# Weight decoding in block 0: cast and split of a piece in one turn, and four attention steps at other places

## The chip, the cores and the metric

The kernel runs on one core of one Trainium2 chip. The metric is the device time of one launch in microseconds (us). TensorE is PE in the profile, VectorE is DVE, ScalarE is ACT, GpSimd is POOL, and SyncE, which issues all the transfers here, is SP. Each of them works through its own queue in order and waits for the others at semaphores.

## What is computed

Three stages follow each other: linear attention over 8 batches of 8 heads (576 tokens, head width 64), a feed-forward layer with `h - tanh(h)`, and a second one with a rational function. The change touches the first two.

```python
q_s = softmax(q, over the 64 entries of a head)
k_s = softmax(k, over the 576 tokens)          # needs the maximum of each column of k
kv  = einsum('bhsd,bhse->bhde', k_s, v)
x   = einsum('bhsd,bhde->bhse', q_s, kv)       # then reshaped to 4608 tokens x 512
h   = x @ w_in                                 # 512 -> 2048
x   = (h - tanh(h)) @ w_out                    # 2048 -> 512
...                                            # second layer: g = P(h) / (Q(h) + 1e-6)
```

## The kernel before

**Blocks and steps.** The 4608 tokens are 9 blocks of 512. The first layer takes 16 steps a block (144 in all, numbered n). Step n forms one 128 x 512 tile `hps` of `h` (`first_product`, 12 matmuls over 4 chunks of 128, each product split in three: high by high, low by high, high by low), takes `t = tanh(hps)` on ACT (L978) and the difference `hps - t` on DVE (L981, called the difference below), rounds it to its high part `gh` on ACT (L336) and forms the rest `gl = g - gh` (L340; on DVE in block 0, on POOL later). Two steps later (`LAG1`) 12 matmuls add it into the four banks `acc` (`second_product1`). There are two `hps` buffers in PSUM. In block 0 the difference is written over `hps` itself, so `hps` of step n comes free for step n + 2 only when `gl` of step n is formed; from block 1 on it is written into `t` in SBUF.

**Decoding.** The weights come as 64-bit floats. In block 0 and shortly before it, 32 pieces of 128 x 512 are decoded (order: a0, a1, b0, a2, b1, a3, ..., a for `w_in`, b for `w_out`). A call of `decode` is a turn; a turn opens one piece (two ACT instructions, L131 and L133, and L134 on DVE), joins the piece opened a turn ago (L146 and L147 on DVE), and handles the one joined before: `dec_high` casts it to the high part on ACT (L154) and `dec_low` splits off the low part (L158), on DVE in a step's first turn and on POOL in its second. In the kernel before, the cast stands last in the turn on ACT, and the split follows one turn later, behind DVE's opening. A step of block 0 has two turns, one ahead of L340 and one behind it; steps 2 and 6 have one. Seven turns lie ahead of step 0.

**Attention steps.** The attention of batch b is cut into four head pairs, and each of its steps is put by hand into a table `work[n]` (L713 to L739). Plain functions stand at the start of step n (`front`, L945), pairs of functions are done where PE turns to them behind the products of step n (`turn`, L976), and their second half behind L340 (`follow`, L990). For keys the steps are `kv_max` (L456 and L457, L461 from batch 2 on), then in batch 1 a transpose on PE with the maximum over it (`kv_turn`, L468; `kv_top`, L474), the way back and the subtraction (`kv_back`, L479; `kv_sub`, L485), the exponential (L495) and the product with the values (`kv_mm`, L515). From batch 2 on the maximum goes through `kv_squares` (L540, L542), a store and a broadcast fetch through memory and `kv_join` (L556). For queries they are `q_max` (L590, DVE), `q_sub` (L595, POOL), `q_exp` (L605, ACT), `q_sum` (L610 to L612 on DVE and L613 on POOL), and the product with `kv` (L660), which ACT copies into `xr` (L674). Behind step 15 `next_x` casts `xr` to `xh` on ACT (L320) and forms `xl` on DVE (L322), on which the first product of block 1 waits.

**Order.** Nothing but the program's own order sets an engine's order (`manual_schedule`). Transfers wait in SP's queue in the order in which they are written.

Of the kernel before, what the change touches and what calls it, by code (L numbers as in the profile page):

```python
# [43 lines left out]
def attention_moe_moe2_kernel(ctx, tc, q, k, v, w1, w2, w3, w4, ca, cb, out):  # L44
# [31 lines left out]
    def f32(ap):  # L76
        return ap.bitcast(F32)
# [27 lines left out]
    staged, joining, parting = [], [], []  # L105
# [43 lines left out]
    def place(piece):  # L149
        which, f = piece  # L150
        return [w[:, f % 4, :] for w in wsl[which, f // 4]]

    def dec_high(piece, m):
        ACT.copy(out=place(piece)[0], in_=f32(m))  # L154

    def dec_low(piece, m, on_dve):
        hi, lo = place(piece)
        (DVE if on_dve else POOL).tensor_tensor(out=lo, in0=f32(m), in1=f32(hi), op=ALU.subtract)  # L158

    def dec_start():  # L160

        old = [joining.pop()] if joining else []
        if staged:
            piece, t = staged.pop(0)
            if wide:
                joining.append((piece, t, *dec_open(t)))
            else:
                old.append((piece, t, None, t))
        return old

    def dec_end(ph, old, low_on_dve):
        if parting and parting[0][2]:
            dec_low(*parting.pop(0)[:2], low_on_dve)
        for x in parting:
            dec_high(*x[:2])
            x[2] = True
        if wide:
            for _, _, e, m in old:
                dec_join(e, m)
        parting.extend([piece, m, False] for piece, _, _, m in old)  # L180
        fetch_w(ph)

    def decode(ph, low_on_dve):
        dec_end(ph, dec_start(), low_on_dve)


# [520 lines left out]
    def put(s, fn, *args):  # L707
        work[max(s, 0)].append((fn, args))

    def first(j):  # L710
        return (j - 1) * KF

    kv_at = {(1, p): 3 * p + 4 for p in range(NPAIR)}  # L713
    q_at = {(1, p): (7, 10, 13, 14)[p] for p in range(NPAIR)}
    for j in range(2, NBLK):
        for p in range(NPAIR):
            q_at[j, p] = first(j) + (8, 8, 14, 14)[p]
            if j < B:
                kv_at[j, p] = first(j) + (8 if p > 1 else 2 if j == 2 else -2)
    q_from = {(j, p): (1, 3, 6, 9)[p] if j == 1 else at - (7 if p % 2 else 10) for (j, p), at in q_at.items()}  # L720
    kv_from = {(b, p): at - (1 if b > 1 and p % 2 else 2) for (b, p), at in kv_at.items()}
    for j in range(1, NBLK):
        for p in range(NPAIR):
            if j < B:
                s, at = kv_from[j, p], kv_at[j, p]
                steps = (s - (2 if p else 1), s - 1, s, s + 1, at) if j == 1 else (s - 3, s - 3, s - 1, s, s, s, at)
                for fn, s in zip(KV if j == 1 else KV_LATER, steps):
                    put(s, fn, j, p)
            s, at = q_from[j, p], q_at[j, p]
            steps = (s - 1, s, s + 1, s + 2, at - 2, at) if j == 1 else (s - 1, s, s + 1, s + 2, s + 3, s + 5, at)  # L730
            for fn, s in zip(Q if j == 1 else Q_LATER, steps):
                put(s, fn, j, p)
        for p in range(2, NPAIR + 2):
            to, before = (j + p // NPAIR, p % NPAIR), (j + (p - 2) // NPAIR, (p - 2) % NPAIR)
            if to in kv_at:
                put(kv_from[before] + 1, load_k, *to)
                put(kv_at[before] + 1, load_v, *to)
            if to in q_at:
                put(q_from[before] + 2, load_q, *to)  # L739

    with tc.manual_schedule():
# [200 lines left out]
        for n in range(STEPS):  # L942
            j, f = n // KF, n % KF
            leave = None
            front(work[n])  # L945
            flush()
            hps = first_product(f)
            if f == KF - 1 and j + 1 < NBLK:
                next_x()
            if n == last:  # L950
                ACT.activation(out=absb, in_=coef[:, 4:6], func=AF.Abs)
                DVE.tensor_scalar(out=coef[:, 0:4], in0=coef[:, 0:4], scalar1=-1.0, scalar2=None, op0=ALU.mult)
            if n == last + 10:
                for errand in todo:
                    for _ in errand:
                        flush()
                flush()
                for pool in (att, bdp, decp, rawp):
                    pool.release()
                outp = ctx.enter_context(tc.tile_pool(name="outp", bufs=4, side="right"))  # L960
                rp = ctx.enter_context(tc.tile_pool(name="rp", bufs=2, side="right"))
                xup = ctx.enter_context(tc.tile_pool(name="xup", bufs=1, side="right"))
                units = [xup.tile([P, NB], F32R, tag=f"u{k}", name=f"u{k}") for k in range(12)]
                units += [w[:, c, :] for w in (xh, xl) for c in range(KC)]
                sums = xup.tile([P, NB], F32, tag="sums", name="sums")
                top = xup.tile([P, HALF], F32, tag="top", name="top")
                temp = xup.tile([P, NB], F32, tag="temp", name="temp")
                for u in range(6):
                    load_unit(0, u)
            if n in due:  # L970
                leave = due.pop(n)()
            if n >= last + LAG1:
                unpark("b", f - LAG1)
            if n > last and f % 4 == 0:
                ring(f // 4 - 1)
            after = turn(work[n])  # L976
            t = gp.tile([P, NB], F32, tag="t", name="t", bufs=1)
            ACT.activation(out=t, in_=hps, func=AF.Tanh)  # L978

            g = t if j else hps  # L980
            DVE.tensor_tensor(out=g, in0=hps, in1=t, op=ALU.subtract)  # L981
            ph_w, turns = None, 0
            if j == 0:
                ph_w, turns = 0, 1 if f in (2, 6) else 2
            gh, gl = split_high(g)
            due[n + LAG1] = lambda a=(j, f, gh, gl): second_product1(*a)
            if turns:
                decode(ph_w, True)
            split_low(g, gh, gl, POOL if j else DVE)
            follow(after)  # L990
            if leave:
                leave()
            if turns > 1:
                decode(ph_w, False)
            if n == KF:
                fetch_w(1)
            if n > KF:
                for errand in todo:
                    next(errand, None)
            if n == STEPS - 1:  # L1000

                ACT.activation(out=ahead, in_=bias_q, func=AF.Abs_reciprocal_sqrt)
# [17 lines left out]
        steps = {f"P{m}": lambda i, m=m: product(i, m) for m in UNITS}  # L1020
# [51 lines left out]
```

## Time and profile before

| | |
|---|---|
| median of 3 runs | 1656.37 us (1656.07 to 1657.74) |
| profiled execution, device time | 1659.01 us |
| its span, first to last instruction | 1657.2 us |
| PE, DVE, ACT, POOL busy, share of the span | 97%, 67%, 62%, 63% |
| PE's granted clock, mean of the span | 0.995 of full |

The profiled execution took 1659.01 us, of which 1657.2 us are the span between its first and its last instruction. The changed places lie in the first 200 us of the span: the attention of block 0 until about 36 us, block 0 of the first layer until about 143 us, and the first steps of block 1. Shares of the whole span say little on them; they are read from stretches of that part, from the list of PE's waits in it and from the instructions in order of time.

### The profile page before, as it was taken

How to read it: one execution, taken by the hardware profiler on the slowest of the kernel's cores; microseconds unless marked ns; L12 is line 12 of the kernel's file. 1: busy time of each engine (PE TensorE's matmuls, PEld its weight loads, DVE VectorE, ACT ScalarE, POOL GpSimd, SP SyncE). 2: the span in 40 equal slices, each digit the busy share in tenths (PEclk: the TensorE clock that was granted, in tenths of full speed). 3: DMA queues.
4: the chain of work that ended last, by engine and by line, in shares of the span. 5: the costliest groups of instructions: out<-in, count | busy, mean ns of one | idle time of the engine just before them, and what ended most of it. 6: DMA issues, size and time to landing. Idle time of an engine off the chain costs nothing.

```text
span 1657.2 us, 26929 instructions
## 1 busy us (share of the span) xinstructions
PE 1613.7 (97%) x9400; PEld 1375.9 (83%) x9400; DVE 1111.3 (67%) x1839; ACT 1023.7 (62%) x1821; POOL 1039.3 (63%) x876
## 2 busy tenths in 40 slices
PE   5899999999999999999999999999999999999998
PEld 3677788888888888887888999898999899999996
DVE  7997656575565656361214787878787787878786
ACT  5675554544545545443325777777777777777775
POOL 4223637375553727273434888888888778778775
PEclk9999999999999999999999999999999999999999
DMA  8563765667473766352387585858686757676640
GB/s 233 174 189 88 208 181 173 182 172 210 135 215 113 222 167 198 107 165 65 121 308 292 173 281 191 291 191 296 196 293 203 267 204 255 214 246 220 209 141 26
DMA packets 250728, 323.75 MB, mean 195 GB/s; under 512 B 119008, under 2 KB 185568, under 8 KB 241376
## 3 DMA queue, kind: packets, MB, share of 16 engines
q1 hardware_dynamic: 250592, 322.03, 61.2%
q8 instruction: 74, 1.21, 0.3%
q14 instruction: 62, 0.51, 0.1%
HBM read 249.04 MB, written 72.93 MB: 194 GB/s over the span
## 4 chain that ended last, share of the span: by engine, by line
PE 86%; DVE 6%; ACT 3%; DMA 3%; issue 1%; SPq 1%; POOL 1%; DVEq 0%; ACTq 0%; POOLq 0%
PE acc L80 14%; PE acc L81 14%; PE acc L82 14%; PE z L866 12%; PE y L866 9%; PE hps L80 7%; PE hps L81 7%; PE hps L82 7%; PE kvps L515 1%; PE xps L660 1%; DVE m L134 1%; DMA u<-x2d 1%; DVE m L147 1%; DMA xh<-x2d 1%; DVE e L146 1%
## 5 line engine op out<-in xcount | busy, mean ns | idle before, releaser
L340 POOL TENSOR_TENSOR gl<-t,gh 128x512 fp32r<-128x512 f32 x128 | 174.5, 1363 | 301.8 <-ACT gh L336 275.8
L923 POOL TENSOR_TENSOR n<-n,r 128x512 f32<-128x512 f32 x144 | 186.3, 1294 | 97.8 <-ACT r L920 92.5
L981 DVE TENSOR_TENSOR t<-hps,t 128x512 f32<-128x512 f32 x128 | 88.1, 689 | 233.0 <-ACT t L978 232.9
L336 ACT CAST gh<-t 128x512 fp32r<-128x512 f32 x128 | 79.7, 622 | 250.3 <-PE acc L82 143.2
L923 POOL TENSOR_TENSOR n<-n,n 128x512 f32<-128x512 f32 x144 | 186.7, 1296 | 36.5 <-ACT n L907 36.5
L923 POOL TENSOR_TENSOR n<-n,h 128x512 f32<-128x512 f32 x144 | 187.6, 1303 | 9.6 <-DMA xl<-x2d 9.6
L978 ACT ACTIVATE t<-hps 128x512 f32<-128x512 f32 x144 | 86.0, 597 | 118.9 <-PE hps L82 86.2
L877 ACT COPY sums<-z 128x256 f32<-128x256 f32 x144 | 53.8, 373 | 134.7 <-PE z L866 134.7
L903 ACT ACTIVATE n<-h,coef 128x512 f32<-128x512 f32 x144 | 116.6, 810 | 0.3 <-POOL n L923 0.3
L933 DVE CAST gh<-a 128x512 fp32r<-128x512 f32 x144 | 99.6, 692 | 16.1 <-PE z L866 0.5
L936 DVE TENSOR_TENSOR gl<-a,gh 128x512 fp32r<-128x512 f32 x144 | 99.6, 692 | 15.5 <-DVE gh L933 0.9
L929 DVE SCALAR_TENSOR_TENSOR a<-a,n 128x512 f32<-128x512 f32 x144 | 100.0, 695 | 14.3 <-POOL n L923 8.5
L912 DVE SCALAR_TENSOR_TENSOR a<-h,absb,a 128x512 f32<-128x512 f32 x144 | 107.6, 747 | 3.0 <-ACT a L897 2.9
L897 ACT ACTIVATE a<-h,coef 128x512 f32<-128x512 f32 x144 | 100.5, 698 | 2.8 <-DVE gl L936 2.8
L926 DVE SCALAR_TENSOR_TENSOR a<-a,r 128x512 f32<-128x512 f32 x144 | 99.4, 690 | 0.8 <-ACT r L920 0.8
L915 ACT ACTIVATE r<-a,bias_q 128x512 f32<-128x512 f32 x144 | 97.1, 674 | 0.0
L920 ACT ACTIVATE r<-r 128x512 f32<-128x512 f32 x144 | 91.1, 632 | 4.6
L900 ACT ACTIVATE h<-h 128x512 f32<-128x512 f32 x144 | 89.2, 619 | 1.0 <-DMA xh<-x2d 0.8
L884 DVE TENSOR_TENSOR h<-y,sums 128x256 f32<-128x256 f32 x72 | 30.6, 425 | 58.4 <-PE y L866 58.4
L888 DVE TENSOR_TENSOR h<-y,top 128x512 f32<-128x512 f32 x72 | 49.7, 691 | 26.5 <-ACT top L877 24.3
L613 POOL TENSOR_TENSOR qe<-qe,qs 128x512 f32<-128x512 f32 x36 | 40.6, 1127 | 40.4 <-DVE qs L612 40.4
L80 PE MATMUL acc<-wb3h,gh 128*128 128x512 f32 x144 | 56.9, 395 | 2.9 <-DVE gh L933 2.9
(296 smaller groups left out, 5114.9 us busy)
## 6 DMA issues: line engine op xcount, KB each, us to landing
u<-x2d SPq DMA_DIRECT2D x78, 256.0 KB, 5.3
raw<-in_moe_w_in_dram SPq DMA_DIRECT2D x32, 512.0 KB, 4.3
raw<-in_moe_w_out_dram SPq DMA_DIRECT2D x32, 512.0 KB, 4.4
x2d<-raw SPq DMA_DIRECT2D x64, 256.0 KB, 3.6
x2d<-xr SPq DMA_DIRECT2D x56, 256.0 KB, 4.0
wa0h<-wa0d SPq DMA_DIRECT2D x9, 1024.0 KB, 5.0
wa1h<-wa2d SPq DMA_DIRECT2D x9, 1024.0 KB, 5.0
wa2h<-wa4d SPq DMA_DIRECT2D x9, 1024.0 KB, 5.1
```

The lines of the kernel that those rows point to most:

```text
L80: PE.matmul(o, lhi, rhi, start=start, stop=False)
L81: PE.matmul(o, lhi, rlo, start=False, stop=False)
L82: PE.matmul(o, llo, rhi, start=False, stop=stop)
L340: eng.tensor_tensor(out=gl, in0=g, in1=f32(gh), op=ALU.subtract)
L866: PE.matmul(o, w, x[:, xc], start=m in (1, 5) and c == k == 0, stop=c == 1 and k == 2, skip_group_check=True,)
L897: ACT.activation(out=new(t, "a", ps_a), in_=t["h"], func=AF.Abs, scale=b0)
L903: ACT.activation(out=new(t, "n1"), in_=t["h"], func=AF.Identity, scale=a3, bias=a2)
L912: DVE.scalar_tensor_tensor(out=t["a"], in0=t["h2"], scalar=b1, in1=t["a"], op0=ALU.mult, op1=ALU.add)
L923: return lambda t: POOL.tensor_tensor(out=t[a], in0=t[a], in1=t[b], op=op)
L929: DVE.scalar_tensor_tensor(out=t["a"], in0=t["a"], scalar=2.0, in1=t["n0"], op0=ALU.subtract, op1=ALU.mult)
L933: DVE.tensor_copy(out=t["g"][0], in_=t["a"])
L936: DVE.tensor_tensor(out=t["g"][1], in0=t["a"], in1=f32(t["g"][0]), op=ALU.subtract)
```

## The change

- **Decoding.** The cast now stands first in a turn on ACT, ahead of the opening's two instructions (`dec_top`), and the split follows in the same turn, behind DVE's join, where it used to follow a turn later. DVE still takes the split of a step's first turn and POOL that of the second; since the split is a turn earlier, the `a` pieces of the early steps now fall to DVE and the `b` pieces to POOL.
- **First pair of batch 1.** Its maximum, transpose, way back and query steps (`q_max`, `q_sub`, ...) move a step later: `kv_max` and `kv_turn` from step 1 to 2, `kv_back` to 3, the exponential to 4, `q_max` from 0 to 2. Its product stays in step 4. The loads that reuse its buffers move by a step too.
- **Batch 2.** The first two `kv_max` move from steps 13 and 14 to 15 and 16, the products from 18 to 19; the query steps of its first pair move two steps later (`q_max` from 13 to 15, `q_exp` from 15 to 17).
- **Step 0.** Its difference is written to `t` in SBUF as in later blocks, so its `hps` comes free right behind the difference.

```diff
+    def dec_top():
+
+        for x in parting:
+            dec_high(*x)
+
     def dec_end(ph, old, low_on_dve):
-        if parting and parting[0][2]:
-            dec_low(*parting.pop(0)[:2], low_on_dve)
-        for x in parting:
-            dec_high(*x[:2])
-            x[2] = True
         if wide:
             for _, _, e, m in old:
                 dec_join(e, m)
-        parting.extend([piece, m, False] for piece, _, _, m in old)
+        while parting:
+            dec_low(*parting.pop(0), low_on_dve)
+        parting.extend((piece, m) for piece, _, _, m in old)
         fetch_w(ph)
 
     def decode(ph, low_on_dve):
+        dec_top()
         dec_end(ph, dec_start(), low_on_dve)
...
-                kv_at[j, p] = first(j) + (8 if p > 1 else 2 if j == 2 else -2)
-    q_from = {(j, p): (1, 3, 6, 9)[p] if j == 1 else at - (7 if p % 2 else 10) for (j, p), at in q_at.items()}
+                kv_at[j, p] = first(j) + (8 if p > 1 else 3 if j == 2 else -2)
+    q_from = {(j, p): (2, 3, 6, 9)[p] if j == 1 else at - (7 if p % 2 else 8 if at == 24 else 10) for (j, p), at in q_at.items()}
...
-                steps = (s - (2 if p else 1), s - 1, s, s + 1, at) if j == 1 else (s - 3, s - 3, s - 1, s, s, s, at)
+                steps = (s - 2, s - 1, s, s + 1, at) if j == 1 and p else (s, s, s + 1, at, at) if j == 1 else (s - 3 + (at == 19), s - 3 + (at == 19), s - 1, s, s, s, at)
...
-            steps = (s - 1, s, s + 1, s + 2, at - 2, at) if j == 1 else (s - 1, s, s + 1, s + 2, s + 3, s + 5, at)
+            steps = (s - (p > 0), s, s + 1, s + 2, at - 2, at) if j == 1 else (s - 1, s, s + 1, s + 2, s + 3, s + 5, at)
...
-                put(kv_from[before] + 1, load_k, *to)
+                put(kv_from[before] + (2 if before == (1, 0) else 1), load_k, *to)
...
-            g = t if j else hps
+            g = t if j or not n else hps
```

Three places show how the queues change. From L187 on, a line of the changed kernel has a number three greater than the same line of the kernel before.

The first is DVE's queue around the maximum of batch 1's first pair (`mx<-kt`), from that maximum on in the kernel before, where it stands ahead of the difference of step 1:

```order
L456 TENSOR_TENSOR mx<-kt_158 128x256
L457 TENSOR_TENSOR mx<-mx,kt_158 128x128
L981 TENSOR_TENSOR hps<-hps,t 128x512
L134 TENSOR_SCALAR m<-raw 128x512
L158 TENSOR_TENSOR wb0l<-m,wb0h 128x512
L146 TENSOR_SCALAR e<-e 128x512
L147 ISA m<-e,m 128x1024
L340 TENSOR_TENSOR gl<-hps,gh 128x512
L474 TENSOR_REDUCE mc<-kvps 128x1
```

And in the changed kernel, from `gl` of step 1 on:

```order
L343 TENSOR_TENSOR gl<-hps,gh 128x512
L134 TENSOR_SCALAR m<-raw 128x512
L146 TENSOR_SCALAR e<-e 128x512
L147 ISA m<-e,m 128x1024
L459 TENSOR_TENSOR mx<-kt_158 128x256
L460 TENSOR_TENSOR mx<-mx,kt_158 128x128
L593 TENSOR_REDUCE qm<-qr 128x8 x2
L984 TENSOR_TENSOR hps<-hps,t 128x512
```

The maximum has moved behind the whole of step 1, two query maxima stand with it, and the split stands behind the join in a first turn.

The second is ACT's queue in step 7, from `gh` on; first the kernel before:

```order
L336 CAST gh<-hps 128x512
L131 ACTIVATE e<-raw 128x512
L133 ACTIVATE m<-raw 128x512
L154 CAST wa2h<-m 128x512
L674 COPY xr<-xps 64x256 x4
L527 ACTIVATE bd_115<-xps,rs 128x64
L131 ACTIVATE e<-raw 128x512
L133 ACTIVATE m<-raw 128x512
L154 CAST wb2h<-m 128x512
```

Then the changed kernel, from the same place:

```order
L339 CAST gh<-hps 128x512
L154 CAST wa2h<-m 128x512
L131 ACTIVATE e<-raw 128x512
L133 ACTIVATE m<-raw 128x512
L677 COPY xr<-xps 64x256 x4
L530 ACTIVATE bd_115<-xps,rs 128x64
L154 CAST wb2h<-m 128x512
L131 ACTIVATE e<-raw 128x512
L133 ACTIVATE m<-raw 128x512
```

The cast that POOL's next split waits for was the fourth row (`wa2h`); now it is the seventh (`wb2h`), behind the four copies.

The third is DVE's queue at the end of block 0; first the kernel before, from the last join on:

```order
L147 ISA m<-e,m 128x1024
L461 TENSOR_REDUCE mx<-kt_159 128x128
L540 STREAM_TRANSPOSE mx<-mx 128x128
L542 TENSOR_REDUCE mc<-mx 128x4
L981 TENSOR_TENSOR hps<-hps,t 128x512
L158 TENSOR_TENSOR wb3l<-m,wb3h 128x512
L340 TENSOR_TENSOR gl<-hps,gh 128x512
L322 TENSOR_TENSOR xl<-xr,xh 128x512 x4
```

Then the changed kernel, from `gl` of step 14 on:

```order
L343 TENSOR_TENSOR gl<-hps,gh 128x512
L464 TENSOR_REDUCE mx<-kt_158 128x128
L543 STREAM_TRANSPOSE mx<-mx 128x128
L545 TENSOR_REDUCE mc<-mx 128x4
L593 TENSOR_REDUCE qm<-qr 128x8
L325 TENSOR_TENSOR xl<-xr,xh 128x512 x4
L984 TENSOR_TENSOR hps<-hps,t 128x512
L343 TENSOR_TENSOR gl<-hps,gh 128x512
```

Of the two maxima of batch 2 one now stands between `gl` of step 14 and the four `xl` of block 1, the other behind them.

## Rows read from the trace of the kernel before

**Rows 1.** Windows by stretch: from:to, length, busy PE, PEld, DVE, ACT, POOL, clock, DMA.

```profile
42.30:50.20 7.90, 0.02 (x1) 0.00 (x0) 7.72 (x13) 4.47 (x8) 2.45 (x2) 0.77 0.54 159
...
54.00:112.00 58.00, 58.00 (x339) 46.68 (x338) 54.72 (x103) 43.61 (x82) 15.22 (x13) 1.00 0.61 185
...
144.00:149.00 5.00, 4.78 (x15) 3.71 (x15) 4.29 (x7) 2.85 (x6) 0.00 (x0) 0.66 0.00 0
```

**Rows 2.** PE's waits, 30 to 240 us: total us, times, longest.

```profile
PE kvps L468 <- DVE mx L456: 7.9, 1, 7.9
...
PE xps L660 <- ACT xr L674: 2.1, 1, 2.1
PE hps L80 <- ACT xh L320: 1.3, 1, 1.3
...
PE qps L619 <- ACT bd L527: 1.0, 1, 1.0
```

**Rows 3.** DVE in order of time, steps 0 to 4: start, duration, line.

```profile
43.21 0.69 DVE L981 TENSOR_TENSOR hps<-hps,t 128x512 f32<-128x512 f32 x1
...
46.41 1.47 DVE L134 TENSOR_SCALAR m<-raw 128x512 uint16<-128x512 uint16 x1
...
49.77 0.42 DVE L456 TENSOR_TENSOR mx<-kt 128x256 f32<-128x256 f32 x1
...
50.43 0.69 DVE L981 TENSOR_TENSOR hps<-hps,t 128x512 f32<-128x512 f32 x1
...
56.83 0.69 DVE L981 TENSOR_TENSOR hps<-hps,t 128x512 f32<-128x512 f32 x1
...
68.99 0.69 DVE L981 TENSOR_TENSOR hps<-hps,t 128x512 f32<-128x512 f32 x1
```

**Rows 4.** POOL in order of time, splits and query subtractions of block 0.

```profile
39.63 1.61 POOL L158 TENSOR_TENSOR wa0l<-m,wa0h 128x512 fp32r<-128x512 f32 x1 [1.52 <-ACT wa0h L154]
...
47.52 1.23 POOL L595 TENSOR_TENSOR qe<-qr,qm 128x512 f32<-128x512 f32 x1
...
80.83 1.24 POOL L595 TENSOR_TENSOR qe<-qr,qm 128x512 f32<-128x512 f32 x1
91.07 1.29 POOL L158 TENSOR_TENSOR wa2l<-m,wa2h 128x512 fp32r<-128x512 f32 x1 [9.01 <-ACT wa2h L154]
...
135.40 1.33 POOL L595 TENSOR_TENSOR qe<-qr,qm 128x512 f32<-128x512 f32 x1
```

**Rows 5.** ACT in order of time, step 7.

```profile
88.68 0.59 ACT L336 CAST gh<-hps 128x512 fp32r<-128x512 f32 x1 [0.82 <-DVE hps L981]
...
90.87 1.53 ACT L674 COPY xr<-xps 64x256 f32<-64x256 f32 x4
92.44 0.32 ACT L527 ACTIVATE bd<-xps,rs 128x64 f32<-128x64 f32 x1
```

**Rows 6.** DVE in order of time, step 7 and the end of block 0.

```profile
87.89 0.70 DVE L981 TENSOR_TENSOR hps<-hps,t 128x512 f32<-128x512 f32 x1 [0.84 <-ACT t L978]
...
92.78 0.46 DVE L134 TENSOR_SCALAR m<-raw 128x512 uint16<-128x512 uint16 x1
...
94.18 0.68 DVE L610 TENSOR_REDUCE qs<-qe 128x8 f32<-128x512 f32 x1
...
128.55 1.29 DVE L461 TENSOR_REDUCE mx<-kt 128x128 f32<-128x640 f32 x1
...
131.02 0.69 DVE L981 TENSOR_TENSOR hps<-hps,t 128x512 f32<-128x512 f32 x1
...
135.86 1.42 DVE L147 CUSTOM_DVE_ANT_0 m<-e,m 128x1024 uint16<-128x1024 uint16 x1
...
139.08 0.69 DVE L981 TENSOR_TENSOR hps<-hps,t 128x512 f32<-128x512 f32 x1
...
143.55 2.50 DVE L322 TENSOR_TENSOR xl<-xr,xh 128x512 fp32r<-128x512 f32 x4 [2.38 <-ACT xh L320]
```

**Rows 7.** Transfers of the batch 2 maxima (`kd`), steps 13 to 22, issue to landing.

```profile
DMA to landing us min/median/max: 1.4/3.4/7.2
```

## The prediction

> **What bounds the kernel now.** I read the stretches of the first 180 us first [rows 1]. From 42.3 to 50.2 us PE does nothing at all while DVE is busy for 7.72 of 7.90 us; from 54 to 112 us PE shows no idle time at the full clock, and DVE is busy for 54.72 of 58.00 us; from 144 to 149 us PE runs at a granted clock of 0.66. Then the list of PE's waits [rows 2]: 7.9 us for the maximum of batch 1's first pair, which stands between two products in PE's queue, 2.1 us for the copies of step 13, 1.3 us for `xh` of block 1, 1.0 us behind step 10. Together 12.3 us, and this is the pot that the change is aimed at. The question is what PE meets when a wait goes, so I read DVE's instructions in order of time [rows 3]. The differences of steps 0, 1, 2 and 4 start at 43.21, 50.43, 56.83 and 68.99 us, and DVE stands idle nowhere between them. So DVE sets the pace of the early steps, and PE's 7.9 us are mostly its lead over DVE: what does not shorten DVE's queue moves that wait and does not remove it.
>
> What stretches DVE's queue is POOL. An opening on DVE takes 0.46 us alone [92.78, rows 6] and 1.47 us where it meets a split on POOL [46.41, rows 3]; a join is held for 1.42 us and ends at 137.28, 0.55 behind POOL's subtraction (135.40 + 1.33) [rows 4, 6]. The other way round POOL waits for DVE's running instruction and then goes ahead of DVE's next one: the split at 39.63 takes 1.61 us where others take 1.29 [rows 4].
>
> The Trainium skill, page "SBUF — State Buffer", section "SBUF: two separate sides", says that VectorE and GpSimd share one pair of ports as an exclusive lock, held for a whole instruction by the one that starts first. By that rule each collision costs in full, which speaks against moving POOL's split behind DVE's opening; the trace agrees (1.47 against 0.46 us), and what the rule makes of the time stands with the second rival.
>
> **Steps 0 to 3.** The sum goes by the start of DVE's differences. Ahead of step 0 a `q_max` (0.6 us) leaves DVE's queue, but ACT's cast of b1 now stands ahead of two openings and waits for its join, so tanh comes later: I take 43.4 against 43.21. A first turn with difference, opening, split, join and `gl` takes 46.41 - 43.21 = 3.2 us [rows 3]; the new order has the same five parts, and the cast on ACT comes in time for a split behind the join, so 3.2 stays. The second turn of step 0 took 49.77 - 46.41 = 3.36 us with two POOL instructions against it, the split and the `q_sub` at 47.52 [rows 3, 4]; now only the split: 1.40 for a turn that nothing holds [92.78 to 94.18, rows 6] and 1.15 for one hold, 2.55. Step 1 then starts at 43.4 + 5.75 = 49.15 and ends at 54.9. Only there stands the moved maximum (0.66, the 50.43 - 49.77 of rows 3): it is ready at 55.6. PE forms `hps` of step 2 from 44.0 (step 0's buffer is free behind the difference: this edit works), adds step 0 into `acc` until about 49.5 (24 matmuls of 0.23), and waits at the transpose until 55.6: **6.1 us in place of 7.9**. Two query maxima (1.2) put step 2 at 56.8, where it was 56.83. Nothing is won. In step 2 the two `q_sub` now run back to back against opening and join, about 1.3 us by the same kind of hold; with the maximum and 0.33 for `kv_top` step 3 starts at 62.2, and with 3.2 + 0.7 (`kv_sub`) + 2.25 + 1.05 (`q_sum`) step 4 at 69.4 against 68.99. **Term 1: +0.45 us**, bounds -1.0 (the tanh isn't late and one `q_sub` misses) to +1.0.
>
> **Steps 4 to 11.** POOL's split used to wait for a cast in the first turn, so it ran beside `gl` and the attention steps on DVE. Step 7 shows it: the split runs from 91.07 to 92.36, DVE's second turn starts at 92.78 and takes 94.18 - 92.78 = 1.40 us, untouched [rows 4, 6]. Now that split waits for the cast of the second turn. ACT reaches it behind the copies and the scaling at 92.44; with 0.2 for the rest of that and the 0.59 that a cast takes [rows 5] it is done at 93.25; POOL asks at 93.3, lets DVE's shift (L146) end at 93.55 and runs until 94.85; the join, due at 93.57 (it is the last 0.6 of the 1.40), ends 0.55 behind that, at 95.4. The queue goes on at 95.3 in place of 94.18: +1.13 us. Step 10 has the same form. In steps 5 and 8 a `q_sub` follows at once on POOL (80.83 for step 5 [rows 4]); it starts 0.9 later with its split, and now holds the join: +0.85 each. In step 4 the join comes 0.1 us too late to be first: +0.76; step 11 +0.2, most of it under a wait for tanh. Steps 6 and 9 keep their lengths. Sum 1.13 x 2 + 0.85 x 2 + 0.76 + 0.2 = 4.9. PE's lead over DVE is small in these steps, so I count all of it as late by step 12. Bounds 0 (POOL slips behind each join) to 4.9. **Term 2: +4.5**, near the upper end because the held opening and the held join in the rows are of this kind; half of step 4 is left out for its margin of 0.1.
>
> **The end of block 0.** Step 13 loses a batch 2 maximum and a `q_max` ahead of its difference: 131.02 - 128.55 = -2.5 [rows 6]. The next step took 139.08 - 131.02 = 8.1 with the second maximum and the join held by `q_sub`; without both it is bound by ACT's copies and takes 5.9: -2.2. So the 2.1 us of PE's wait for these copies go. But one maximum and the `q_max` now stand between `gl` of step 14 and `xl`: 3.1 + 2.5 = 5.6 from difference to `xl` where it was 143.55 - 139.08 = 4.5: +1.1. **Term 3: -3.6.** The edit takes one of the two maxima past `xl`, not both. Right behind that `q_max` POOL's `q_sub` of batch 2 is ready and can hold the second `xl`: 0 to 1.25 us, **term 4: +0.6**. The clock of 0.66 in 144 to 149 us costs 5.0 x 0.34 = 1.7 us [rows 1]; it came behind PE's waits there, and PE will still wait some 1 us for `xl`, so I take half back: **term 5: -0.85**, bounds -1.7 and 0.
>
> **Block 1** I cost at nothing: its second maximum now has two steps rather than three until its join, with a store and a fetch between (median landing 3.4, longest 7.2 us [rows 7]) against steps of some 6 us (68.99 - 43.21 over four, rows 3); PE's lag of two steps covers a late fetch. Without that cover it costs up to 3 us. The moved loads wait for buffers that are free when SP reaches them, and behind them SP holds only weight pieces that wait for an opening anyway.
>
> **Sum.** 0.45 + 4.5 - 3.6 + 0.6 - 0.85 = **+1.1 us**. On the span of 1657.2 that is 1658.3; the profiled execution took 1659.01 with its ends, 2.6 above the median 1656.37, so I put the sum on the median: **1657.5 us**.
>
> **The rivals.** First, the waits are really removed because **POOL does not hold the joins**: term 2 is 0, term 4 is 0, term 5 is -1.7: 0.45 - 3.6 - 1.7 = -4.9, 1651.5 us. For it: POOL and DVE ask within 0.1 to 0.3 us of each other in these steps. Against it: the 1.61 us of the split at 39.63. Second, **slower: POOL's splits hold DVE in full and are themselves stretched**, in the second turns of steps 0 to 11: 4.9, and some 0.3 more in eight collisions (1.61 against 1.29), 2.4, with term 4 at 1.25 and no clock regained: 0.45 + 4.9 + 2.4 - 3.6 + 1.25 = +5.4, 1661.8 us. It decides from about 1.2 us a colliding step on. The Trainium skill's lock rule, named above, would bring this case; the 1.61 us is the one row here that bears out its second half. Third, **DVE is not the pace but PE's waits are**: then 7.9 - 6.1, 2.1, 1.3, 1.0 and 1.7 of clock all come back, -7.9, 1648.5 us. Against it stands DVE without idle time between the differences [rows 1, 3].
>
> **How the numbers follow.** A measurement of this kernel can tell about 0.2%, 3.3 us, from no change. My forecast, within 0.2% either way: 0.43, its own range 1653.5 to 1659.6. POOL does not hold: 0.24. PE's waits come back: 0.09. Slower: 0.24. So faster 0.33, same 0.43, slower 0.24. The range 1650.5 to 1661.5 leaves out most of the third rival and the upper half of the slower one.
>
> **What would show it.** In the changed profile: PE's wait for the first maximum at 5 to 7 us rather than gone (step by step right; under 2 us would refute the pace by DVE); the join of steps 7 and 10 at 1.5 us and more in place of 0.69 (term 2); the difference of step 13 within 1.5 us of 133, and new short waits of PE for `gl` in steps 8 to 12; no wait for the copies of step 13; `xl` of block 1 at 144 to 146 us, behind a maximum. If `xl` starts before 141 us, term 2 is wrong; if PE waits in steps 17 to 20, the nothing for block 1 is.

## The result and the profile after

The changed kernel takes **1664.47 us** (median of 4 runs, 1663.0 to 1665.29) against 1656.22 us for the kernel before on the same chip (4 runs, 1653.5 to 1657.74). The ratio is 1.0051, 95% interval 1.0033 to 1.0068: slower by about 8 us, where I had forecast 1657.5 us and a range that ended at 1661.5. The profiled execution of the changed kernel took 1663.0 us, its span 1661.2 us. In the changed kernel the difference is L984, `gl` L343 and `xl` L325; the join stays L147.

Where did the time go? I compare milestones. The first is the first `xl` subtraction of block 1: 143.55 us before, 145.05 after, so block 0 costs 1.5 us. The second is the same instruction for block 2: 239.65 before, 245.56 after, so block 1 costs 4.4 us more. From there to the ninth block nothing changes: the last `xl` stands at 789.05 before and 794.91 after, still 5.9 us. The loss thus arises in the first 245 us, and most of it in block 1, which I had put at nothing. The second and the last milestone, before (L322) and after (L325):

```profile
239.65 2.50 DVE L322 TENSOR_TENSOR xl<-xr,xh 128x512 fp32r<-128x512 f32 x4 [1.63 <-ACT xh L320]
...
789.05 2.50 DVE L322 TENSOR_TENSOR xl<-xr,xh 128x512 fp32r<-128x512 f32 x4 [5.41 <-ACT xh L320]
```

```profile
245.56 2.50 DVE L325 TENSOR_TENSOR xl<-xr,xh 128x512 fp32r<-128x512 f32 x4 [1.64 <-ACT xh L323]
...
794.91 2.50 DVE L325 TENSOR_TENSOR xl<-xr,xh 128x512 fp32r<-128x512 f32 x4 [5.41 <-ACT xh L323]
```

PE's waits from 30 to 240 us in the changed kernel (engine, tile and line, releaser: total us, times, longest us), the answer to [rows 2]:

```profile
PE hps L80 <- DVE t L984: 5.3, 2, 4.1
PE kvps L471 <- DVE mx L459: 5.1, 1, 5.1
PE xps L650 <- ACT bd L533: 2.5, 1, 2.5
PE hps L80 <- DVE gl L343: 2.1, 4, 1.2
...
PE hps L81 <- DVE xl L325: 1.2, 2, 0.7
```

The first maximum's wait has shrunk from 7.9 to 5.1 us, and the 2.1 us for the copies of step 13 are gone. New are short waits for `gl`, and one wait of 4.1 us for `t`, where the list before had two waits of 0.8 us together. It lies in block 1. (The 2.5 us for `bd`, 1.0 before, stand at 34.6 us, ahead of step 0.) DVE's milestones in block 0 (start, duration, line), the answer to [rows 3] and [rows 6]:

```profile
74.81 1.71 DVE L147 CUSTOM_DVE_ANT_0 m<-e,m 128x1024 uint16<-128x1024 uint16 x1
...
95.69 1.67 DVE L147 CUSTOM_DVE_ANT_0 m<-e,m 128x1024 uint16<-128x1024 uint16 x1
...
118.26 1.67 DVE L147 CUSTOM_DVE_ANT_0 m<-e,m 128x1024 uint16<-128x1024 uint16 x1
...
127.70 0.69 DVE L984 TENSOR_TENSOR hps<-hps,t 128x512 f32<-128x512 f32 x1
...
133.51 0.70 DVE L984 TENSOR_TENSOR hps<-hps,t 128x512 f32<-128x512 f32 x1 [1.03 <-ACT t L981]
...
139.41 0.70 DVE L984 TENSOR_TENSOR hps<-hps,t 128x512 f32<-128x512 f32 x1 [0.34 <-ACT t L981]
...
145.05 3.33 DVE L325 TENSOR_TENSOR xl<-xr,xh 128x512 fp32r<-128x512 f32 x4
```

The joins of steps 4, 7 and 10 take 1.67 to 1.71 us in place of 0.69. The difference of step 12 comes at 127.70 (122.72 before), that of step 13 at 133.51 (131.02), that of step 14 at 139.41 (139.08). The lag of 5 us that the decoding builds up by step 12 is nearly caught up by step 14, and comes back in part ahead of `xl`.

The wait of 4.1 us has a chain behind it that goes through five queues. All engines but PE in order of time, steps 16 to 19 of the changed kernel (SPq is SP issuing a transfer; in brackets the idle time before and its releaser):

```profile
153.38 1.09 DVE L559 TENSOR_REDUCE mx<-qe 128x128 f32<-128x512 f32 x1
...
154.50 0.32 SPq L553 DMA_DIRECT2D qe<-kd  x1
...
157.53 0.62 ACT L339 CAST gh<-t 128x512 fp32r<-128x512 f32 x1 [1.35 <-DVE raw L811]
...
159.84 1.07 DVE L559 TENSOR_REDUCE mx<-qe 128x128 f32<-128x512 f32 x1
...
160.99 1.68 POOL L598 TENSOR_TENSOR qe<-qr,qm 128x512 f32<-128x512 f32 x1 [5.45 <-DVE mx L559]
...
162.63 1.28 POOL L343 TENSOR_TENSOR gl<-t,gh 128x512 fp32r<-128x512 f32 x1
...
163.95 0.60 ACT L981 ACTIVATE t<-hps 128x512 f32<-128x512 f32 x1 [0.61 <-POOL gl L343]
...
164.58 0.69 DVE L984 TENSOR_TENSOR t<-hps,t 128x512 f32<-128x512 f32 x1 [2.81 <-ACT t L981]
```

PE at the end of that chain, in the same kernel:

```profile
173.83 0.79 PE L80 MATMUL hps<-xh,wa1h 128*128 128x512 f32 x1 [4.14 <-DVE t L984]
```

The chain reads as follows. For batch 1 and later there are two tiles with the tag `qe`. `kv_fetch` puts the broadcast maxima of a key pair into one, and `q_sub` of the queries writes into the same ring. The join of pair 0 (L559, 153.38) frees a tile; only then does SP issue the fetch of pair 1 (154.50); its join runs at 159.84 to 160.91; and only that frees the tile for `q_sub` of query pair 1, which POOL had at the head of its queue and for which it stood idle 5.45 us (160.99). The place in the program matters more than the fetch: the change puts the join of pair 1 from step 17 into step 18 and leaves this `q_sub` in step 17, so the head of POOL's queue waits for an instruction that DVE reaches a step later. The tile kept the fetch of pair 1 waiting for some 0.8 us only, since the store ahead of it went out at 152.30 and took 1.4 us to land. Behind that `q_sub` in POOL's queue stands `gl` of step 17. Its input `gh` was done at 158.15 (157.53 + 0.62), but it starts at 162.63, 4.5 us late. `gl` reads `t`, of which there is one buffer, so the tanh of step 18 waits for it (163.95), and so does its difference (164.58). DVE's queue then holds 8.5 us of work up to the difference of step 19 at 173.09, and PE waits for that. Some 2.8 us of these look like holds by POOL, which works off its backlog beside them: the shift (L146) takes 1.27, the join 1.66 and L614 1.17 us, where 0.41, 0.69 and 0.17 stand elsewhere in this trace. Before the change the same `q_sub` ran at 154.16, right behind `gl` of step 16, and `gl` of step 17 at 157.59.

The wait also costs clock. Windows of the changed kernel (from:to, length, busy PE, PEld, DVE, ACT, POOL, granted clock, DMA):

```profile
143.00:153.00 10.00, 8.79 (x38) 6.63 (x37) 9.16 (x15) 3.60 (x7) 1.28 (x1) 1.00 0.15 26
153.00:163.00 10.00, 10.00 (x46) 8.26 (x45) 8.37 (x12) 5.54 (x10) 3.30 (x3) 1.00 0.36 93
163.00:173.00 10.00, 6.69 (x64) 5.38 (x62) 8.24 (x11) 3.30 (x6) 8.57 (x7) 0.93 0.37 123
173.00:190.00 17.00, 16.17 (x62) 13.19 (x63) 9.58 (x16) 8.72 (x17) 12.33 (x11) 0.84 0.67 187
```

The same windows of the kernel before:

```profile
143.00:153.00 10.00, 9.20 (x32) 7.21 (x33) 8.57 (x15) 4.67 (x10) 1.15 (x2) 0.83 0.23 62
153.00:163.00 10.00, 10.00 (x68) 8.13 (x68) 4.95 (x7) 6.11 (x11) 5.52 (x4) 1.00 0.43 138
163.00:173.00 10.00, 10.00 (x64) 8.31 (x60) 8.34 (x17) 4.18 (x9) 5.85 (x5) 1.00 0.35 78
173.00:190.00 17.00, 17.00 (x77) 14.08 (x76) 9.83 (x11) 6.17 (x12) 14.12 (x13) 1.00 0.86 226
```

Before, PE stood idle 0.8 us of these 47 and the clock was low at their start. After, it stood idle 5.35 us, and the clock fell behind the wait: 0.93, then 0.84 for the 17 us in which PE was busy again.

### The profile page after: what moved, and what is told of

It is laid out like the page before. It is cut to its first block, busy times and chain, and to the rows that moved or that the text cites. A ratio compares the mean times of both kernels' runs of the same rounds, so it can differ in the third digit from the quotient of the medians.

```text
span 1661.2 us, 26925 instructions
## 1 busy us (share of the span) xinstructions
PE 1615.7 (97%) x9400; PEld 1376.2 (83%) x9400; DVE 1113.1 (67%) x1839; ACT 1024.2 (62%) x1821; POOL 1041.3 (63%) x876
## 4 chain that ended last, share of the span: by engine, by line
PE 89%; DVE 6%; ACT 3%; DMA 1%; issue 1%; SPq 1%; POOL 0%; DVEq 0%; ACTq 0%; POOLq 0%
PE acc L80 15%; PE acc L81 15%; PE acc L82 15%; PE z L869 12%; PE y L869 9%; PE hps L80 7%; PE hps L81 7%; PE hps L82 7%; PE xps L663 1%; PE kvps L518 1%; DVE m L147 1%; DVE m L134 1%; ACT m L133 1%; DVE xl L325 0%; DVE hps L984 0%
## 5 line engine op out<-in xcount | busy, mean ns | idle before, releaser
L343 POOL TENSOR_TENSOR gl<-t,gh 128x512 fp32r<-128x512 f32 x128 | 174.0, 1360 | 304.6 <-ACT gh L339 280.8
L984 DVE TENSOR_TENSOR t<-hps,t 128x512 f32<-128x512 f32 x129 | 88.7, 687 | 227.6 <-ACT t L981 227.6
L900 ACT ACTIVATE a<-h,coef 128x512 f32<-128x512 f32 x144 | 100.5, 698 | 2.6 <-DVE gl L939 2.6
L147 DVE CUSTOM_DVE_ANT_0 m<-e,m 128x1024 uint16<-128x1024 uint16 x64 | 60.5, 946 | 3.4
L80 PE MATMUL hps<-xh,wa1h 128*128 128x512 f32 x144 | 57.5, 399 | 4.5 <-DVE t L984 4.1
```

The lines of the kernel that those rows point to most:

```text
L80: PE.matmul(o, lhi, rhi, start=start, stop=False)
L343: eng.tensor_tensor(out=gl, in0=g, in1=f32(gh), op=ALU.subtract)
L900: ACT.activation(out=new(t, "a", ps_a), in_=t["h"], func=AF.Abs, scale=b0)
```

## Experiments

The theory: the decode edit costs what its held joins cost (A1), and the batch 2 edit makes the wait in block 1 through the shared tile (A). The rival B: that wait is an echo of the decoding's lag. I took the change apart first. All times are medians; the ratio is against the kernel before on the same chip, with its 95% interval.

| kernel | `xl` of block 1 | of block 2 | time, us | ratio |
|---|---|---|---|---|
| before, two traces | 143.55, 143.20 | 239.65, 240.08 | 1656.2 to 1657.15 | 1 |
| changed | 145.05 | 245.56 | 1664.47 | 1.0051 [1.0033, 1.0068] |
| e1_no_b2 | 147.60 | 241.80 | 1659.96 | 1.0020 [1.0011, 1.0029] |
| e2_b2_only | 138.53 | 239.60 | 1658.33 | 1.0016 [1.0007, 1.0025] |
| e3_dec_only | 147.44 | 241.79 | 1659.70 | 1.0023 [1.0014, 1.0032] |
| e5_first_only | 142.79 | 237.78 | 1656.97 | 1.0003 [0.9994, 1.0012] |
| e6_behind_gl | 145.26 | 245.46 | 1663.77 | 1.0041 [1.0028, 1.0053] |
| e6_qsub_late | 144.66 | 244.18 | 1663.21 | 1.0042 [1.0028, 1.0055] |
| e7_swap | 142.24 | 236.51 | 1654.54 | 0.9990 [0.9981, 0.9998] |
| e8_swap_late | 139.33 | 239.06 | 1656.32 | 0.9999 [0.9991, 1.0008] |
| e9_swap_only_dec | 143.63 | 237.74 | 1656.80 | 1.0000 [0.9991, 1.0010] |
| e11_b2_behind_gl | 138.57 | 238.41 | 1655.83 | 0.9998 [0.9989, 1.0007] |
| e12_b2_first_behind_gl | 138.75 | 239.25 | 1656.68 | 0.9998 [0.9989, 1.0007] |

### e1_no_b2: the change without its batch 2 edit

```diff
-                kv_at[j, p] = first(j) + (8 if p > 1 else 3 if j == 2 else -2)
+                kv_at[j, p] = first(j) + (8 if p > 1 else 2 if j == 2 else -2)
-    q_from = {(j, p): (2, 3, 6, 9)[p] if j == 1 else at - (7 if p % 2 else 8 if at == 24 else 10) for (j, p), at in q_at.items()}
+    q_from = {(j, p): (2, 3, 6, 9)[p] if j == 1 else at - (7 if p % 2 else 10) for (j, p), at in q_at.items()}
-                steps = (s - 2, s - 1, s, s + 1, at) if j == 1 and p else (s, s, s + 1, at, at) if j == 1 else (s - 3 + (at == 19), s - 3 + (at == 19), s - 1, s, s, s, at)
+                steps = (s - 2, s - 1, s, s + 1, at) if j == 1 and p else (s, s, s + 1, at, at) if j == 1 else (s - 3, s - 3, s - 1, s, s, s, at)
```

> The changed kernel with the batch 2 edit taken back: batch 2's first two maxima in block 0 again, one step earlier than in the changed kernel. Theory A (the wait of 4.1 us at 173.8 us is made by the batch 2 edit: the fetch of pair 1 comes late, the q_sub behind it waits for the tile that both use, and gl, tanh and DVE's queue wait behind that): the wait in steps 19 to 21 is gone, block 1 takes what it takes in the kernel before (xl of block 1 to xl of block 2: 96.1 us against 100.5 in the changed kernel); block 0 on the other hand gets the maxima back and keeps the decode's held joins, xl of block 1 at 147 to 149 us against 145.05. Sum about +4 to +5 us over the kernel before, 1660 to 1661.5 us: within 1 or 2 us of the changed kernel. Theory B (that wait is an echo of the decode, whose held joins bring DVE late and without slack into block 1): the wait stays, at 3 us or more, and the time is 1664 to 1668 us.

Measured: 1659.96 us, `xl` of block 1 at 147.60, block 1 (`xl` to `xl`) 94.2 us. PE's waits from 143 to 240 us are these and no others:

```profile
PE hps L80 <- ACT xh L323: 0.6, 1, 0.6
PE hps L80 <- DVE t L984: 0.5, 2, 0.3
PE hps L81 <- DVE xl L325: 0.2, 1, 0.2
```

The wait of 4.1 us is gone although the decoding is late as ever. Rival B falls. Block 1 is even 1.9 us shorter than before: PE comes into it at full clock (1.00 from 147 to 152 us, against the 0.66 of 144 to 149 us before).

### e2_b2_only: the kernel before with the batch 2 edit

The edit is the inverse of the diff of e1, put into the kernel before.

> The kernel before with the batch 2 edit alone. Theory A: the wait of about 4 us in steps 19 to 21 appears, xl of block 1 to xl of block 2 takes about 100 us in place of 96.1; block 0 loses maxima ahead of xl, so that xl of block 1 comes at 140 to 142 us in place of 143.55; sum +1 to +2 us, 1657 to 1659 us. Theory B: no such wait, block 1 at 96 to 97 us, the gain of block 0 stays, 1652 to 1654 us.

Measured: 1658.33 us. Block 0 gains 5.0 us (`xl` at 138.53), block 1 takes 101.1 us, 5.0 more than before. The two sum to nothing at block 2. PE's waits from 143 to 245 us in this kernel:

```profile
PE hps L80 <- DVE t L981: 4.8, 1, 4.8
```

POOL in order of time, the `q_sub` that waits (line numbers of before):

```profile
155.11 1.68 POOL L595 TENSOR_TENSOR qe<-qr,qm 128x512 f32<-128x512 f32 x1 [6.07 <-DVE mx L556]
156.75 1.29 POOL L340 TENSOR_TENSOR gl<-t,gh 128x512 fp32r<-128x512 f32 x1
```

The wait and its chain appear with this edit alone, without any of the decoding's lag.

### e3_dec_only: the kernel before with the decode edit

The edit is the part of the change's diff in `dec_top`, `dec_end` and `decode`.

> The kernel before with the edit of the decoding alone. My term 2 (POOL's split holds the joins in steps 4 to 11): held joins of 1.5 to 1.7 us, xl of block 1 at 147 to 149 us in place of 143.55, block 1 as before with 96 us; 1659.5 to 1661.5 us. Rival (the holds are swallowed by waits that stand there anyway): xl at 143 to 145 us, 1656 to 1658 us. Theory B: a wait of 3 us or more in steps 19 to 21, 1662 us or more.

Measured: 1659.70 us, ratio 1.0023. `xl` of block 1 is 3.9 us late (147.44), within the bounds of my term 2, and no long wait stands in block 1 (0.6 us at most). Block 1 gives back 1.75 us (94.35 against 96.10).

### e5_first_only: first pair and step 0 alone

The edit is the change's lines on batch 1 (`q_from` and `steps` for `j == 1`, `load_k`) and `g = t if j or not n else hps`.

> The kernel before with the two small edits alone: first pair of batch 1 a step later, and step 0's difference in SBUF. By my working DVE sets the pace of steps 0 to 4, so PE's wait for the first maximum gets shorter (about 5 to 6 us in place of 7.9) without anything coming earlier: 1655.5 to 1657 us, the difference of step 4 at 68.5 to 69.5 us against 68.99. Rival (PE's wait is the pace): 1653 to 1654.5 us, the difference of step 4 before 67.5 us.

Measured: 1656.97 us, ratio 1.0003, no difference that can be told. PE's wait for the first maximum is 5.5 us in place of 7.9, and the difference of step 4 starts at 68.23 (68.99 and 68.41 in the two traces of before). DVE is the pace there, as worked out.

### e6_behind_gl: one exchange on POOL in the changed kernel

```diff
             for fn, s in zip(Q if j == 1 else Q_LATER, steps):
-                put(s, fn, j, p)
+                put(s, (nothing, fn) if fn is q_sub and (j, p) == (2, 1) else fn, j, p)
```

> The changed kernel with two instructions of POOL exchanged: the q_sub of batch 2's second query pair stands behind gl of step 17 and not ahead of it; nothing else moves on any engine. Theory A (gl of step 17 is held because it stands behind a q_sub that waits for the tile of the fetched maxima): the wait of 4.1 us in steps 19 to 21 goes or falls under 1 us, xl of block 2 comes at 241 to 242.5 us against 245.56, the time is 1660 to 1661.5 us. Rival C (DVE's own queue in steps 17 and 18, with joins held by POOL and a maximum, is the cause, and gl would have been late anyway): 3 us or more of wait stay, 1663.5 to 1665 us.

Measured: 1663.77 us, `xl` of block 2 at 245.46: nothing won, with 3.2 us of PE's wait left. POOL and ACT in order of time show why:

```profile
162.11 1.69 POOL L598 TENSOR_TENSOR qe<-qr,qm 128x512 f32<-128x512 f32 x1 [2.37 <-DVE mx L559]
...
163.83 0.63 ACT L608 ACTIVATE qe<-qe 128x512 f32<-128x512 f32 x1 [2.62 <-POOL qe L598]
...
164.37 0.58 ACT L981 ACTIVATE t<-hps 128x512 f32<-128x512 f32 x1
```

`gl` of step 17 is on time now (158.45). But the `q_sub` still waits for the tile, its exponential stands in ACT's queue ahead of the tanh of step 18, and the tanh starts at 164.37 in place of 163.95. The join of pair 1 that it waits for also comes later, at 160.98 in place of 159.84: DVE's opening at 158.64 now meets `gl` on POOL and takes 1.42 us in place of 0.47. My expectation of 1660 to 1661.5 was wrong by naming one queue. The time lies where rival C, DVE's own queue, had put it, but C alone is not it either: DVE stands idle for 2.2 us ahead of that step's difference at 165.05.

### e6_qsub_late: the whole query chain a step later

```diff
-    q_from = {(j, p): (2, 3, 6, 9)[p] if j == 1 else at - (7 if p % 2 else 8 if at == 24 else 10) for (j, p), at in q_at.items()}
+    q_from = {(j, p): (2, 3, 6, 9)[p] if j == 1 else at - (6 if at == 24 and p == 1 else 7 if p % 2 else 8 if at == 24 else 10) for (j, p), at in q_at.items()}
```

> The changed kernel with the whole chain of batch 2's second query pair (q_max, q_sub, its exp and all that follows up to the fetch) one step later. Behind gl alone, the q_sub still held ACT: its exp stands ahead of the tanh of step 18 and waited for it until 163.83 us. Theory A (the late tile of the fetched maxima is the cause, and it holds whatever stands behind its user on POOL or on ACT): the difference of step 18 comes at 158 to 161 us in place of 164.58, the wait of 3 to 4 us is gone, xl of block 2 at 241 to 242.5 us, 1660 to 1661.5 us. Rival C (DVE's own queue of steps 18 and 19 is the cause): the wait stays, 1663 us or more.

Measured: 1663.21 us. The difference of step 18 comes at 162.66 in place of 164.58, that of step 19 at 168.13 in place of 173.09, and the wait in steps 19 to 21 is gone. But `xl` of block 2 gains only 1.4 us (244.18), because a wait of 2.73 us stands later, in block 1 still. DVE and PE in order of time:

```profile
189.82 1.10 DVE L559 TENSOR_REDUCE mx<-qe 128x128 f32<-128x512 f32 x1 [4.46 <-DMA qe<-kd]
```

```profile
194.03 0.50 PE L80 MATMUL hps<-xh,wa2h 128*128 128x512 f32 x1 [2.73 <-DVE t L984]
```

This is the join of batch 3's first pair. It waits for its fetch, which SP issued at 185.61, behind four fetches of the batch 2 queries (182.03 to 184.76) and a store; in the kernel before one such fetch went out at 179.81, ahead of the four query fetches at 185.15. So the step that was too tight was moved, not taken away.

### e11_b2_behind_gl and e12_b2_first_behind_gl: the batch 2 edit without the decode edit, with the exchange

The edits are that of e2 with the exchange of e6_behind_gl; in e12 the first pair and step 0 are changed as well.

> The kernel before with the batch 2 edit and the same exchange on POOL. Theory A: block 0's gain of 5 us (xl of block 1 at 138.5 us in place of 143.55) is kept through block 1, xl of block 2 at 235 to 236.5 us against 239.6; time 1652.5 to 1654.5 us, faster than the kernel before by 2 to 4 us. Rival C: xl of block 2 at 239 us or later, 1657 to 1659 us.

> The changed kernel without its decode edit and with the exchange on POOL: all that is left is the first pair a step later, step 0's difference in SBUF, and batch 2's maxima later. Theory A: 1651.5 to 1654 us, xl of block 2 at 233.5 to 236 us, the best of these kernels. If the first-pair edit's gain of 1 to 2 us in its own run does not add: as the kernel before with the batch 2 edit and the exchange.

Measured: 1655.83 and 1656.68 us, both 0.9998 of before: no difference. Block 1 takes 99.8 and 100.5 us. The gain of 5 us in block 0 isn't carried through block 1 by the exchange. Both expectations of a faster kernel were wrong, for the reason that e6_behind_gl shows: in e11 the `q_sub` waits 2.37 us for the join (155.43), and the tanh starts at 157.69, behind its exponential.

### e7_swap: the engines of the two splits exchanged

```diff
             if turns:
-                decode(ph_w, True)
+                decode(ph_w, turns < 2)
...
             if turns > 1:
-                decode(ph_w, False)
+                decode(ph_w, True)
```

This is e1_no_b2 with these lines: in a step with two turns POOL takes the first turn's split and DVE the second's.

> The changed kernel without the batch 2 edit, and the engines of the two splits of a step exchanged: the first turn's on POOL (where a step has two turns), the second turn's on DVE. If the 3.3 us that the decode edit costs are joins held by POOL's split in the second turn (my term 2), joins in steps 5, 7, 8 and 10 take their 0.69 again and xl of block 1 comes at 143 to 145 us (147.60 with the splits as the change has them), time 1656 to 1658 us. Rival (the cost is the order itself: cast and split in one turn make every turn wait for the cast, whichever engine splits): xl at 147 us or later, 1659.5 us or more.

Measured: **1654.54 us**, ratio 0.9990 [0.9981, 0.9998]. It is 5.4 us under e1 and the only kernel here that is faster than before. All joins from 42 to 146 us (count, busy us and mean ns), before:

```profile
L147 DVE CUSTOM_DVE_ANT_0 m<-e,m 128x1024 uint16<-128x1024 uint16 x27 | 19.4, 719 | 2.0
```

in the changed kernel, with the openings under it:

```profile
L147 DVE CUSTOM_DVE_ANT_0 m<-e,m 128x1024 uint16<-128x1024 uint16 x27 | 26.7, 987 | 2.0
...
L134 DVE TENSOR_SCALAR m<-raw 128x512 uint16<-128x512 uint16 x25 | 14.4, 575 | 0.0
```

and in e7:

```profile
L147 DVE CUSTOM_DVE_ANT_0 m<-e,m 128x1024 uint16<-128x1024 uint16 x27 | 19.8, 734 | 1.9
```

From 41 to 146 us the changed kernel has nine joins of over 1.2 us, e7 has one (41.49, ahead of step 0) and the first trace of before has one. With the splits exchanged POOL's runs in the first turn, behind that turn's join and beside `gl` (0.68 us at 70.53 and 77.42, not held), and the joins of the steps are free.

### e9_swap_only_dec: the exchange without the other edits

The edit is the decode edit with the exchange of e7, in the kernel before.

> The kernel before with the decode edit alone and the engines of its two splits exchanged (first turn's on POOL, second turn's on DVE). With the splits as the change has them this was 1659.7 us and xl of block 1 came at 147.44. If the held joins are all that the decode edit costs: joins (L147) at 0.69 us in most steps and a mean under 0.8 us, xl of block 1 at 142 to 144 us, xl of block 2 at 236.5 to 238.5 us, time 1653.5 to 1656 us, about 5 us under the edit as it stands. If the gain of the exchange in the other kernel came from the first pair's move beside it: xl of block 1 at 146 us or later, 1658 us or more.

Measured: 1656.80 us, 2.9 us under e3 (by the ratios, each against before on its own chip, 0.23% or 3.8 us); joins at a mean of 733 ns, `xl` of block 1 at 143.63 and of block 2 at 237.74, as expected. The time itself is a little over the 1653.5 to 1656 that I had put, and equal to the kernel before. So the exchange takes back the cost of the decode edit with or without the first pair's move.

### e8_swap_late: everything, with the exchange and the query chain late

The edits of e7 (the exchange) and of e6_qsub_late, in the changed kernel whole.

> The changed kernel whole, with the engines of the two splits exchanged (which, with batch 2 as before the change, brought xl of block 1 to 142.24 us and the time to 1654.5 us) and that query chain one step later. If both causes are right and add: xl of block 1 at 138 to 141 us, xl of block 2 at 233 to 236 us, time 1650 to 1654 us, under every kernel so far. If the batch 2 edit costs in block 1 what it gains in block 0 by more than this chain: xl of block 2 at 236.5 us or later, 1654 to 1657 us.

Measured: 1656.32 us, ratio 0.9999. `xl` of block 1 at 139.33 is as hoped, `xl` of block 2 at 239.06 is not: block 1 takes 99.7 us, and the gain of the exchange is spent there.

### b_again: the kernel before, a second trace

> The kernel before once more, unchanged, for a second trace. In nine kernels the time differs from the kernel before by 1 to 2.7 us more than xl of block 2 does in the traces, always to the same side. If that is the one profiled execution of before, which took 1659.01 us against a median of 1656.4: here the span is shorter, and xl of block 2 comes 1 to 2.5 us before 239.65. If it lies behind block 2 (something that every changed kernel loses in the later blocks): xl of block 2 at 239 to 240 us again.

Measured: 1657.05 us, `xl` of block 2 at 240.08, of the last block at 789.49, span 1655.3. The first trace had 789.05 and 1657.2. So the first layer repeats within 0.45 us, and from the last `xl` to the end the same kernel took 868.15 us once and 865.8 once. The explanation that the first trace of before was late in the first layer falls.

## Why the prediction was wrong

**Block 0 came out as it was worked.** The difference of step 4: +0.61 us, term 1 had +0.45. By step 12: +4.98, terms 1 and 2 had +4.95. The end of the block: step 12 to 13 in 5.81 us in place of 8.30 (-2.5), 13 to 14 in 5.90 in place of 8.06 (-2.2), 14 to `xl` in 5.64 in place of 4.47 (+1.2); term 3 had -2.5, -2.2 and +1.1. At `xl` that is +1.50, where the terms gave +1.35. Term 4, the second `xl` held by `q_sub`: the four take 3.33 in place of 2.50, +0.83; the term had +0.6. Term 5: the clock of 0.83 in 143 to 153 us is 1.00 now, 1.7 us and not the half of it that I took. The joins of steps 7 and 10 at 1.67 us, the first maximum's wait at 5.1, `xl` behind a maximum at 145.05 are as forecast. Of the joins that were named, steps 4, 5, 7, 8 and 10 are held; those of steps 0 and 1 (1.58 at 47.72, 1.54 at 53.30) and of step 9 (1.57 at 110.81) are as well, and step 11's is not.

One held join in its rows, POOL's split, ACT's cast for it, and DVE's join in step 4:

```profile
74.68 1.30 POOL L158 TENSOR_TENSOR wa1l<-m,wa1h 128x512 fp32r<-128x512 f32 x1 [3.81 <-DVE e L146]
```

```profile
73.99 0.61 ACT L154 CAST wa1h<-m 128x512 fp32r<-128x512 f32 x1
```

```profile
73.92 0.46 DVE L134 TENSOR_SCALAR m<-raw 128x512 uint16<-128x512 uint16 x1
74.27 0.41 DVE L146 TENSOR_SCALAR e<-e 128x512 uint32<-128x512 uint32 x1
74.81 1.71 DVE L147 CUSTOM_DVE_ANT_0 m<-e,m 128x1024 uint16<-128x1024 uint16 x1
```

The split starts at 74.68, 0.08 behind the end of its cast (74.60) and as DVE's shift (L146) ends, so ahead of the join, which ends at 76.52, 0.54 behind the split's end (75.98); the sum had used 0.55. In step 7 the split starts at 95.45, also 0.08 behind its cast and while the shift still runs (95.24 to 95.65), and again the join behind the shift is the one held. The Trainium skill, page "SBUF — State Buffer", section "SBUF: two separate sides", calls this an exclusive lock of VectorE and GpSimd that the first to start holds for a whole instruction; the trace agrees with it for these joins. For the other direction, POOL held by DVE, this split of 1.30 us shows nothing; the 1.61 us of [rows 4] bear it out.

**The step that failed is "Block 1 I cost at nothing".** It cost 5.9 - 1.5 = 4.4 us by the second milestone, although the clock at its start gave 1.7 us back. I had asked whether the fetched maxima land in time for their join, found PE's lag of two steps enough for that, and put "up to 3 us" as the price of a late fetch, which I then left out of the sum and out of the range's upper end. What I didn't ask is who else uses the tile that the fetch fills. The diff moves the maxima by two steps, their joins by one and the second `q_sub` by none, and both take their tile from one ring of two. So the wait isn't PE's or DVE's for the maxima, it is POOL's for a buffer, and behind POOL's head stands `gl`. e1 and e2 show it from both sides: without the batch 2 edit no such wait, with that edit alone 4.8 us of it.

**The batch 2 edit moves work, it does not save any.** Alone it takes 5.0 us out of block 0 and puts 5.0 us into block 1. In all seven kernels with it, block 1 takes 99.5 to 101.1 us; in the seven traces without it, 94.1 to 96.9. e6_behind_gl, e6_qsub_late and e8 moved the waiting instruction behind `gl`, then behind the tanh, and each time the next user in a queue came late: the exponential, then the fetch of batch 3. That the `q_sub` waits for the tile is firm: in the changed kernel, e2, e6_behind_gl and e11 it starts 0.07 to 0.08 us behind the end of the join, and the tile is all that the two have in common. By this account a third tile of the ring, or the `q_sub` behind the join in the program with its later steps moved along, would take the wait away; the first was not tried, and the second, e6_qsub_late, brought a new wait. So that the ring is the whole cause of the 5 us is argued from this chain, and not shown.

**The second rival had the right sign for another reason.** It put the loss at block 0: splits stretched in eight collisions, and no clock. The decode edit does cost, 1.0023 alone, but that is 3.9 us at `xl` against the 4.5 of my term 2, not more. Taken one by one the three edits give 0.23%, 0.16% and 0.03%, together 0.42% or 7.0 us; the whole gave 0.51% with an interval from 0.33% to 0.68%.

**What stays open.** The milestones account for 5.9 us, the medians differ by 8.2. For the changed kernel by itself 5.9 us, 0.36%, are still inside the interval; but the difference goes the same way in every kernel of the table: e5 and e9 reach block 2 about 2 us earlier than before and take as long, e2 reaches it at the same time and takes 0.16% more. b_again shows that the first layer of before isn't the reason; what is left is the second layer, which neither the change nor any of these edits touches and which took 865.8 and 868.15 us in two traces of one kernel. In the changed kernel's trace it took 866.3 us, between these two, so no trace shows that the change loses there. I didn't find what in it varies.

## What to carry to other kernels

When a step is moved, list the tiles that it takes and who else takes tiles from the same ring: a buffer that comes free later stops the next user at the head of its queue, and everything behind that, even on an engine that the diff does not name. Look for the instruction that frees the tile: if the move puts it into a later step than the one that waits, the wait is built in. A saving at one milestone counts only when the next milestone keeps it, so read the milestones on both sides of the place that the work is moved to. Where two engines hold each other's instructions, try which of two neighbouring turns each of them takes before moving the work in time: here that exchange was worth 0.23% in one kernel (e9 against e3) and 0.30% in another (e7 against e1), 4 to 5 us, about what the decode edit had cost.

## What the hardware showed beyond that

A single wait of PE costs more than its length. In the changed kernel the granted clock was 1.00 through the 20 us ahead of the wait of 4.14 us, 0.93 in the ten in which it lies and 0.84 in the 17 after it, which are nearly all work again: 16.17 us busy at 0.84 is some 2.6 us of work not done. In e2, behind its wait of 4.8 us, it is 0.90 from 168 to 190 us; in e1, without such a wait, 1.00 from 147 to 190 us. In e6_qsub_late, without that wait, the clock from 154.66 to 189.66 us is 1.00, and it falls to 0.89 in the 15 us with the later wait.

And the turn in which POOL's split runs decides whether a join is held: with it in the second turn eight joins of steps 0 to 10 are held, with it in the first turn none, and the mean of 27 joins is 734 ns in place of 987. I had priced the hold (0.55 us behind POOL's end; here 0.54), but not seen that the same two splits, the other way round, cost nothing that can be told (e9, 1.0000 of before).
